# An attention and gated-MLP kernel on one core: query product units begin in odd blocks, their steps at other positions, and the score tiles stand ahead of the values while a unit holds a PSUM pair

## The chip, the core and the metric

The kernel runs on one core of a Trainium2 chip. A core has TensorE (matrix products into PSUM, its weights loaded by a separate queue that the profile calls PEld), VectorE (DVE), ScalarE (ACT), GpSimd (POOL) and SyncE (SP, which issues the transfers). Each engine takes its instructions in the order of the program and stops at one whose semaphore hasn't come yet. The metric is the device time of one execution in microseconds, lower is better. Times below are in microseconds from the first instruction of the profiled execution where they stand as positions.

## The reference

Two parts share a layer norm of `x` (2048 rows of 512). `A` is attention of 32 heads of 128 over a cache of 2048 keys, without a mask; `B` is a gated MLP with relu on the gate.

```python
def _A_ref(x, k_cache, v_cache, wq, wo):
    q = (x @ wq).reshape(B, Sq, H, Dh).transpose(0, 2, 1, 3)
    scores = jnp.einsum("bhqd,bhkd->bhqk", q, k_cache) * (Dh ** -0.5)
    p = _softmax(scores, axis=-1)
    o = jnp.einsum("bhqk,bhkd->bhqd", p, v_cache)
    return o.transpose(0, 2, 1, 3).reshape(B, Sq, H * Dh) @ wo

def _B_ref(x, W_gate, W_up, W_down):
    gate = x @ W_gate
    h = gate * (gate > 0) * (x @ W_up)
    return h @ W_down

xn = _layernorm(A_x)
out = A_x + _A_ref(xn, ...) * silu(_B_ref(xn, ...))
```

## The kernel before, in words

**The main loop.** The attention is cut into 128 *blocks*, one for each head and quarter of the queries (512 rows); `blk_of` gives block, head, quarter and *position*. A block has 8 positions, each a *pair* of key tiles (2 x 128 keys). For a pair, TensorE makes two score tiles (`emit_S_tile`, line 1461) into one PSUM pair, ScalarE takes the exponential of both in one instruction (line 1473) into `PT`, and later TensorE multiplies both tiles with the values (`emit_PV_tile`, line 1570, eight matmuls a pair) into the accumulator `ps_acc`. The values run three pairs behind the scores (`LAG`): an iteration of the loop opens pair `gp` and does the values of pair `gq = gp - 3`. At a block's end VectorE normalizes the accumulator (`emit_norm_block`, a reciprocal at line 1490 and a product at line 1493), and the next block's first value matmul waits for that.

**The ring.** Six PSUM banks, as three pairs, are handed out in turn by `ring_acquire` to pairs of score tiles and to side products. A pair comes back when the exponential has read it, or when VectorE has read a side product. `ring_acquire(hold=True)` takes a pair out of the turn, and `ring_release` puts it back as the next but one; meanwhile two pairs are left for the scores.

**Side products.** What else TensorE has to do is spread over the iterations by a plan written out by hand, `plan[(block, position)]`, and short pieces of other engines by `side[(block, position)]`. In an iteration with items of the plan, both score tiles come first, then the items, then the values. In one without, the order is score tile, half of the values, score tile, half of the values. Blocks in `early` have a product that takes only one bank at position 0; there the next pair's two score tiles are opened ahead of it as well, and position 1 opens none.

- *Output products* (`emit_os`, line 1342): the output projection of a finished group of four heads (16 blocks), as seven products for each of four quarters, spread over the 16 blocks of the next group, one step at position 0 of each. Each fourth step is a single bank; its blocks (3, 7, 11 and 15 of a group) are the early ones. VectorE adds the results to `s_acc` (line 1360).
- *Output sums* (`emit_ox`, lines 1311 to 1319): sums and differences of attention outputs that these products read, four VectorE operations each for the first half (`c = 0`, read from block 1 on) and the second half (`c = 1`, read from block 9 on). They are written into one buffer, `OX`.
- *Weight sums for them* (`emit_wx`, GpSimd): one scaling and four sums per group.
- *Query product units* (`emit_unit`, line 1027): the queries of head group `g` are made by two nested levels of a seven-product scheme, in the 16 blocks before they are used. A group has seven units (`j` = 1, 2, 6, 5, 3, 7, 4), each again of seven products in six steps. Steps 0 to 3 share one held pair of banks: step 0 makes two products, the others one; a step often waits for VectorE's result of the step before (`k["b"]`, `k["a"]`), since it accumulates on a bank that VectorE has just read. Steps 4 and 5 hold a pair again, in the next block. VectorE does two operations each for steps 0 and 1 and one for each of the others (lines 1031 and 1032); in step 1 of the units that add to a base (all but `j` = 1 and 5) the second is of double width, 128x1024. `prep_unit` makes a unit's operand sums on GpSimd (line 999) two blocks ahead, and `add_unit` adds two buffers on GpSimd after units 5 and 7.

`unit_at` lists where units begin: before, in blocks 6, 8, 10, 12, 14 of a group and 0 and 2 of the next (even blocks), with steps at positions 2, 4, 5, 6 of that block and 2, 4 of the next. There are units for six groups, from block 22 to block 115. The first two groups' queries are made by a simpler scheme, `emit_st`: its step 0 copies a product from PSUM to the buffer `cu` on VectorE (line 909).

Of the kernel before, what the change touches and what calls it, by code (L numbers as in the profile page):

```python
# [30 lines left out]
def _wait(eng, tok):  # L31
    if tok is None:
        return
    sem, val = tok
    if val <= 0:
        return
    eng.wait_ge(sem.h, val)


def _wait_all(eng, toks):  # L40
    best = {}
    for t in toks:
        if t is None:
            continue
        sem, val = t
        k = id(sem)
        if k not in best or best[k][1] < val:
            best[k] = (sem, val)
    for sem, val in best.values():
        _wait(eng, (sem, val))  # L50


def bass_recurrent_scan__mha_block_cached__glu_gated_reglu__prompt_kernel(
# [24 lines left out]
    NP = KT // 2  # L78
# [3 lines left out]
    NG = H // G  # L82
# [29 lines left out]
    act = nc.scalar  # L112
    dve = nc.vector
# [3 lines left out]
    with ExitStack() as es:  # L117
# [9 lines left out]
        def newsem(unit=1):  # L127
            _cnt[0] += 1
            return _Sem(es.enter_context(nc.semaphore(f"sem{_cnt[0]}")), unit)

        ps_r = P_([128, 2 * NSLOT, 512], F32, "ps_r")
# [136 lines left out]
        sem_g = newsem()  # L268
        sem_qpe = newsem()
        sem_da = newsem()  # L270
        sem_rz = newsem()
        sem_norm = newsem()
        sem_opa = newsem()
# [589 lines left out]
        GBK = G * QB  # L863
# [9 lines left out]
        st_tok = {}  # L873

        def emit_st(pr, c, step, *banks):
            W, X = Wq_sb[pr % 2], SW[pr % 2] if pr else SW0
            cu, cv = cuv0 if pr == 0 and c == 0 else cuv
            lo = slice(c * NQ, (c + 1) * NQ)
            hi = slice(HS + c * NQ, HS + (c + 1) * NQ)
            h0, h1 = 2 * pr, 2 * pr + 1  # L880
            Q0, Q1 = c, c + QB // 2

            def prod(k, bank):
                L, R = {
                    1: (lambda i: W[:, i, 0, :], lambda i: xnT[:, i, lo]),
                    2: (lambda i: W[:, HC + i, 0, :], lambda i: xnT[:, HC + i, lo]),
                    3: (lambda i: X[:, 3, i, :], lambda i: xnT[:, HC + i, hi]),
                    4: (lambda i: W[:, HC + i, 1, :], lambda i: TX[:, 3, i, lo]),
                    5: (lambda i: X[:, 0, i, :], lambda i: TX[:, 0, i, lo]),
                    6: (lambda i: X[:, 1, i, :], lambda i: TX[:, 1, i, lo]),  # L890
                    7: (lambda i: X[:, 2, i, :], lambda i: TX[:, 2, i, lo]),
                }[k]
                ins = None
                for i in range(HC):
                    ins = pe.matmul(ps_r[:, bank, :], L(i), R(i), start=(i == 0), stop=(i == HC - 1))  # L895
                return sem_qp.sig(ins)

            def comb(dst, a, bank, op=ALU.add, waits=()):
                _wait_all(dve, waits)
                return sem_qpe.sig(dve.tensor_tensor(dst, a, ps_r[:, bank, :], op))  # L900

            if step == 0:
                _wait(pe, sw_tok[(pr, 0)])
                if pr == 0 and c == 0:
                    _wait_all(pe, xt_ready[0])
                p1 = prod(1, banks[0])
                p2 = prod(2, banks[1])
                _wait(dve, p1)
                st_tok["u"] = sem_qpe.sig(dve.tensor_copy(cu[:], ps_r[:, banks[0], :]))
                r = qt_ready[(h0, Q0)] = comb(qt_take(h0, Q0), cu[:], banks[1], waits=(p2, st_tok["u"]))  # L910
                return [st_tok["u"], r]
            if step == 1:
                if c == 0:
                    _wait(pe, sw_tok[(pr, 1)])
                    _wait(pe, tx_tok[(1, 3)])
                p6 = prod(6, banks[0])
                p5 = prod(5, banks[1])
                st_tok["u"] = comb(cu[:], cu[:], banks[0], waits=(p6, st_tok["u"]))
                st_tok["v"] = comb(cv[:], cu[:], banks[1], waits=(p5, st_tok["u"]))
                return [st_tok["v"]]  # L920
            if step == 2:
                p3 = prod(3, banks[1])
                p7 = prod(7, banks[0])
                qt_ready[(h0, Q1)] = comb(qt_take(h0, Q1), cv[:], banks[1], waits=(p3, st_tok["v"]))
                st_tok["u"] = comb(cu[:], cu[:], banks[0], waits=(p7, st_tok["u"]))
                r = qt_ready[(h1, Q1)] = comb(qt_take(h1, Q1), cv[:], banks[0])
                return [r]
            p4 = prod(4, banks[0])
            if c == 1:
                qp_done_tok[pr] = p4  # L930
            r = qt_ready[(h1, Q0)] = comb(qt_take(h1, Q0), cu[:], banks[0], waits=(p4, st_tok["u"]))
            st_tok["r"] = r
            return [r]

        qp3 = {18: ((1, 0), (3, 1), (5, 2)), 19: ((0, 3), (2, 4), (4, 5)), 20: ((3, 6), (5, 7))}
        unit_at = [(g, j, GBK * (g - 1) + 6 + 2 * k) for g in range(2, NG)
                   for k, j in enumerate((1, 2, 6, 5, 3, 7, 4))]
        u_prep = {}
        u_done = {}
# [1 line left out]
        u_held = {}  # L941
# [699 lines left out]
        GB = G * QB  # L1641
        LB = NBLK - QB
        side = {}
        osteps = {}
        early = set()
        for g in range(NG - 1):
            b0 = (g + 1) * GB
            for i in range(16):
                it = (emit_os, 1 if i % 4 == 3 else 2, g, i // 4, i % 4)
                if g < NG - 2 or i < 10:  # L1650
                    osteps[b0 + i] = it
                else:
                    at(b0 + (10, 10, 11, 12, 13, 13)[i - 10], 4 * (i in (11, 15)), it)
            for c in range(2):
                for i in range(4):
                    side.setdefault((b0 + 7 * c, (2, 1)[c] + i), []).append((emit_ox, g, c, i))
        gu_n = [len(gu_seq)]

        def gu_items(n):
# [17 lines left out]
        for b in range(NBLK):  # L1677
            pr, r = (b - 2) // 8 + 1, (b - 2) % 8
# [22 lines left out]
            elif 0 < pr < NPR:  # L1701
                c, step = r // 4, r % 4
                q = (emit_st, 1 if step == 3 else 2, pr, c, step)
                first, second = (o, q) if step == 3 and o else (q, o)
# [3 lines left out]
            else:  # L1708
                assert not o
        for n, (g, j, b) in enumerate(unit_at):  # L1710
            for step, (r, p) in enumerate(((0, 2), (0, 4), (0, 5), (0, 6), (1, 2), (1, 4))):
                at(b + r, p, (emit_unit, 0, n, step))
            side.setdefault((b - 2, 0), []).append((prep_unit, n))
            if j in (5, 7):
                side.setdefault((b + 1, 5), []).append((add_unit, g, j))
        side.setdefault((GB + 1, 0), []).append((spill_g,))
        side.setdefault((LB - 9, 5), []).append((reload_g,))
        for g in range(2, NG):
            b = GB * (g - 1)
# [35 lines left out]
        for gp in range(LAG, TOTP):  # L1755
            gq = gp - LAG
            bq, hq, Qq, pq = blk_of(gq)
            items = plan.pop((bq, pq), None)
            b, h, Q, p = blk_of(gp)
            if p == 0 and Q == 0:  # L1760
                sp_head_start(h)
            ahead = gp in s_ahead
            if not ahead:
                open_S_pair(gp)
                emit_S_tile(gp, 0)
            if pq == 0 and bq % 8 == 4:
                pr = bq // 8 + 2
                if pr < 4:
                    _wait(sp, qp_done_tok[pr - 2])
                    issue_wq(pr)  # L1770
            if pq == 4 and bq % 8 == 4:
                pr = bq // 8 + 2
                if pr < 4:
                    emit_sw(pr)
            if pq == 0 and bq == (NG - 1) * GB + 4:
                _wait(sp, u_tok["last"])
                for k in range(4):
                    issue_xr(k)
            if pq == 4 and bq == 0:
                gu_sums(2)  # L1780
            if pq == 0 and bq == 13:
                emit_wx_scale(0)
            if pq == 0 and bq == GB:
                emit_wx(0)
            if pq == 0 and bq == GB + 3:
                emit_wx(1)
            if pq == 6 and bq % GB == 8 and 1 < bq // GB < NG - 1:
                emit_wx(bq // GB)
            if items:
                if not ahead:  # L1790
                    emit_S_tile(gp, 1)
                if pq == 0 and bq in early:
                    s_ahead.add(gp + 1)
                    emit_S_pair(gp + 1)
                for it in items:
                    emit_M(it)
            for fn, *args in side.pop((bq, pq), []):
                fn(*args)
            for fn in later.pop(gq, []):
                fn()  # L1800
            now[0] = gq + 1
            emit_PV_tile(gq, 0)
            if not items and not ahead:
                emit_S_tile(gp, 1)
            emit_PV_tile(gq, 1)

# [40 lines left out]
```

## Time and profile before

| | |
|---|---|
| time, median of 3 runs | 1265.59 us (1265.51 to 1265.65) |
| time of the profiled execution | 1265.56 us |
| its span, first to last instruction | 1264.2 us |
| TensorE clock granted | 0.999 |
| exponentials, line 1473 | 1024, mean 1029 ns, 982.6 us busy |
| value matmuls, line 1570 | 8192 |
| VectorE operations of units, 128x512, line 1032 | mean 685 ns |
| the same, double width 128x1024 | mean 1220 ns |
| additions to the output, line 1360 | 264, mean 683 ns |

In a row of the timeline the columns are: start, length, engine, line, operation, written tile <- read tiles, shapes, how many were merged; in brackets, how long the engine stood idle before it and who ended that. The idle time of PE is that against the ends of the records; a matmul's record goes on after the next one has begun, so a stall shows in the distance between starts, not in the bracket. In rows that list one group of instructions, the numbers are shortest, median and longest duration in ns, then the first and last start.

### The profile page before, as it was taken

How to read it: one execution, taken by the hardware profiler on the slowest of the kernel's cores; microseconds unless marked ns; L12 is line 12 of the kernel's file. 1: busy time of each engine (PE TensorE's matmuls, PEld its weight loads, DVE VectorE, ACT ScalarE, POOL GpSimd, SP SyncE). 2: the span in 40 equal slices, each digit the busy share in tenths (PEclk: the TensorE clock that was granted, in tenths of full speed). 3: DMA queues.
4: the chain of work that ended last, by engine and by line, in shares of the span. 5: the costliest groups of instructions: out<-in, count | busy, mean ns of one | idle time of the engine just before them, and what ended most of it. 6: DMA issues, size and time to landing. Idle time of an engine off the chain costs nothing.

```text
span 1264.2 us, 29137 instructions
## 1 busy us (share of the span) xinstructions
PE 1238.9 (98%) x12124; PEld 856.6 (68%) x12353; DVE 804.9 (64%) x1329; ACT 1033.6 (82%) x1108; POOL 588.5 (47%) x606
## 2 busy tenths in 40 slices
PE   9999999999999999999999999999999999999998
PEld 5466666776767676667766677767666676766775
DVE  7677887765566646664665646564655656565667
ACT  4457877668888898888888898888888898889994
POOL 3473876315525366254654457335645447430002
PEclk9999999999999999999999999999999999999999
DMA  9712331315212332323212223233223132235312
GB/s 271 154 31 43 71 80 29 45 43 126 39 35 48 75 60 47 51 64 68 52 37 47 53 60 51 51 64 67 48 51 65 30 56 47 51 66 140 76 35 76
DMA packets 254914, 82.25 MB, mean 65 GB/s; under 512 B 226368, under 2 KB 254784, under 8 KB 254784
## 3 DMA queue, kind: packets, MB, share of 16 engines
q1 hardware_dynamic: 254112, 79.98, 30.8%
q8 instruction: 98, 1.61, 0.5%
q10 hardware_dynamic: 672, 0.39, 0.1%
q14 instruction: 32, 0.26, 0.1%
HBM read 40.63 MB, written 4.19 MB: 35 GB/s over the span
## 4 chain that ended last, share of the span: by engine, by line
PE 80%; issue 8%; ACT 7%; DVE 3%; POOL 0%; DMA 0%; POOLq 0%; DVEq 0%
PE ps_acc L1570 31%; PE ps_r L1461 26%; ACT PT L1473 7%; PE ps_r L1027 6%; PE ps_r L1342 6%; PE ps_r L1139 3%; PE ps_r L1200 2%; PE ps_r L710 2%; PE ps_r L714 2%; PE ps_r L895 2%; DVE UVR L1032 1%; PE ps_acc L813 1%; POOL g_sb L1625 0%; DVE OX L1319 0%; DVE OX L1313 0%
## 5 line engine op out<-in xcount | busy, mean ns | idle before, releaser
L1473 ACT ACTIVATE PT<-ps_r 128x1024 bf16<-128x1024 f32 x1024 | 982.6, 1029 | 161.3 <-PE ps_r L1461 148.5
L1570 PEld LDWEIGHTS ps_acc<-V_sb,PT 128*128 128x128 bf16 x8192 | 589.2, 98 | 199.5 <-ACT PT L1473 2.9
L1570 PE MATMUL ps_acc<-V_sb,PT 128*128 128x129 bf16 x8192 | 715.7, 220 | 7.1
L1461 PE MATMUL ps_r<-QT_sb,KT_sb 128*128 128x512 bf16 x1835 | 626.1, 379 | 8.6 <-DVE UVR L1032 5.4
L1032 DVE TENSOR_TENSOR UVR<-UVR,ps_r 128x512 f32<-128x512 f32 (+1 forms) x228 | 168.2, 755 | 89.7 <-PE ps_r L1027 86.8
L1461 PEld LDWEIGHTS ps_r<-QT_sb,KT_sb 128*128 128x128 bf16 x2048 | 179.5, 98 | 14.2 <-DVE UVR L1032 5.1
L1360 DVE TENSOR_TENSOR s_acc<-s_acc,ps_r 128x512 f32<-128x512 f32 x264 | 167.8, 683 | 21.9 <-PE ps_r L1342 21.9
L1490 DVE RECIPROCAL rz_sb<-ps_acc 128x4 f32<-128x4 f32 x127 | 23.2, 182 | 217.0 <-PE ps_acc L1570 216.9
L999 POOL TENSOR_TENSOR TI<-xn_sb 128x512 f16<-128x512 f16 x48 | 55.3, 1153 | 113.3 <-PE ps_r L1027 113.3
L1493 DVE TENSOR_TENSOR Onorm<-ps_acc,rz_sb 128x512 bf16<-128x512 f32 x127 | 87.8, 691 | 4.4
L999 POOL TENSOR_TENSOR TI<-xnT 128x512 f16<-128x512 bf16 x36 | 41.5, 1154 | 69.6 <-PE ps_r L1027 68.8
L973 POOL TENSOR_SCALAR Wq_sb<-Wq_sb 128x1024 bf16<-128x1024 bf16 x12 | 33.2, 2768 | 83.5 <-DMA Wq_sb<-in_A_wq_dram 83.5
L1032 DVE TENSOR_TENSOR QT_sb<-UVR,ps_r 128x512 bf16<-128x512 f32 x72 | 47.9, 686 | 36.6 <-PE ps_r L1027 34.2
L1098 POOL TENSOR_TENSOR QT_sb<-UVR,UVR 128x512 bf16<-128x512 f32 x24 | 29.8, 1274 | 81.8 <-DVE UVR L1032 81.8
L1098 POOL TENSOR_TENSOR UVR<-UVR,UVR 128x512 f32<-128x512 f32 x24 | 29.8, 1272 | 73.3 <-DVE UVR L1032 73.3
L1625 POOL TENSOR_TENSOR g_sb<-s_acc,WX 128x512 bf16<-128x512 f32 x6 | 6.8, 1153 | 117.3 <-DVE WX L1618 117.3
L999 POOL TENSOR_TENSOR TI<-xn_sb,TI 128x512 f16<-128x512 f16 x48 | 55.4, 1154 | 0.0
L1027 PE MATMUL ps_r<-TI,SI 128*128 128x512 f16 x126 | 48.0, 381 | 0.6
L1342 PE MATMUL ps_r<-WX,OX 128*128 128x256 f16 x336 | 45.8, 273 | 0.0
L999 POOL TENSOR_TENSOR TI<-xnT,TI 128x512 f16<-128x512 bf16 x36 | 41.6, 1157 | 0.0
L1115 POOL TENSOR_SCALAR gB<-gB 128x512 bf16<-128x512 bf16 x14 | 20.8, 1487 | 42.4 <-DVE gB L1145 42.4
L1342 PEld LDWEIGHTS ps_r<-WX,OX 128*128 128x128 f16 x336 | 32.9, 98 | 9.8 <-ACT PT L1473 1.8
(185 smaller groups left out, 1191.2 us busy)
## 6 DMA issues: line engine op xcount, KB each, us to landing
V_sb<-in_A_v_cache_dram SPq DMA_DIRECT2D x32, 512.0 KB, 4.5
Wq_sb<-in_A_wq_dram SPq DMA_DIRECT2D x16, 256.0 KB, 3.1
Wo_sb<-in_A_wo_dram SPq DMA_DIRECT2D x8, 512.0 KB, 4.9
out_dram<-g_sb SPq DMA_DIRECT2D x4, 512.0 KB, 4.8
g_sb<-out_dram SPq DMA_DIRECT2D x4, 512.0 KB, 6.6
xr_sb<-in_A_x_dram SPq DMA_DIRECT2D x16, 128.0 KB, 2.2
OT_store<-Onorm SPq DMA_TRANSPOSE x127, 2.5
Wd_sb<-in_B_W_down_dram SPq DMA_DIRECT2D x1, 1792.0 KB, 14.6
```

The lines of the kernel that those rows point to most:

```text
L973: wu_tok[(g, i)] = sem_uo.sig(pool.tensor_scalar(w, w, WSC, None, op0=ALU.mult))
L999: return sem_ui.sig(pool.tensor_tensor(dst, x, y, o))
L1027: return sem_up.sig(pe.matmul(dst, lhs, rhs, start=start, stop=stop, skip_group_check=True))
L1032: dve.tensor_tensor(dst, x, ps, ALU.add))
L1098: u_tok["add"] = sem_uv.sig(pool.tensor_tensor(dst, UU[:, i, :], RR[:, i, :], ALU.add))
L1139: ins = pe.matmul(ps_r[:, bank, :], L(i), R(i), start=(i == 0), stop=(i == HC - 1))
L1342: ins = pe.matmul(ps_r[:, bank, j * DH:(j + 1) * DH], L(i), R(i), start=(i == 0 and j == 0), stop=(i == GH - 1 and j == 1))
L1360: t = dve.tensor_tensor(names[k], names[k], view(bank), op)
L1461: ins = pe.matmul(ps_r[:, 2 * s + tt, :], KT_sb[h % 2][:, t * 128:(t + 1) * 128], QT_sb[qt_slot[(h, Q)]][:], start=True, stop=True)
L1473: act.activation(PT[pb][:], ps_r[:, 2 * s:2 * s + 2, :], ACTF.Exp, scale=scale / WSC)
L1493: dve.tensor_tensor(Onorm[ob][:], o_ap, rz_sb[:].to_broadcast([128, 4, Dh]), ALU.mult))
L1570: ins = pe.matmul(o_ap, PT[pb][:, tt, j * 128:(j + 1) * 128], V_sb[vb][:, t, 0:VW], start=(t == 0 and j % 2 == 0), stop=(t == KT - 1 and j ...
```

## The change

Six edits to the order of work; no product is added or left out.

1. `emit_st`, step 0 of head pair 0, second column: the copy to `cu` is done by ScalarE, not VectorE (once in the program).
2. Units begin one block earlier, in odd blocks (5, 7, 9, 11, 13, 15 and 1).
3. Their first four steps are at positions 2, 3, 5, 6, or 3, 4, 6, 7 in early blocks, in place of 2, 4, 5, 6. The last two stay at 2 and 4 of the next block.
4. The output sums of the second half move from block 7, positions 1 to 4, to block 8, positions 2 to 5 (except in the last group).
5. `emit_wx` of group 1 comes a block later, those of later groups a block earlier.
6. In an iteration without items, both score tiles come ahead of the values while a unit holds a pair, and at position 7 ahead of an early block.

```diff
@@ emit_st, step 0
-                _wait(dve, p1)
-                st_tok["u"] = sem_qpe.sig(dve.tensor_copy(cu[:], ps_r[:, banks[0], :]))
+                if pr == 0 and c == 1:
+                    _wait_all(act, [p1, st_tok["r"]])
+                    st_tok["u"] = sem_qpa.sig(act.copy(cu[:], ps_r[:, banks[0], :]))
+                else:
+                    _wait(dve, p1)
+                    st_tok["u"] = sem_qpe.sig(dve.tensor_copy(cu[:], ps_r[:, banks[0], :]))
@@ 
-        unit_at = [(g, j, GBK * (g - 1) + 6 + 2 * k) for g in range(2, NG)
+        unit_at = [(g, j, GBK * (g - 1) + 5 + 2 * k) for g in range(2, NG)
                    for k, j in enumerate((1, 2, 6, 5, 3, 7, 4))]
@@ 
             for c in range(2):
                 for i in range(4):
-                    side.setdefault((b0 + 7 * c, (2, 1)[c] + i), []).append((emit_ox, g, c, i))
+                    side.setdefault((b0 + 7 * c, 1 + i) if c and g == NG - 2 else (b0 + 8 * c, 2 + i), []).append((emit_ox, g, c, i))
@@ 
         for n, (g, j, b) in enumerate(unit_at):
-            for step, (r, p) in enumerate(((0, 2), (0, 4), (0, 5), (0, 6), (1, 2), (1, 4))):
+            first = (3, 4, 6, 7) if b in early else (2, 3, 5, 6)
+            for step, (r, p) in enumerate([(0, p) for p in first] + [(1, 2), (1, 4)]):
                 at(b + r, p, (emit_unit, 0, n, step))
@@ the loop
-            if pq == 0 and bq == GB + 3:
+            if pq == 0 and bq == GB + 4:
                 emit_wx(1)
-            if pq == 6 and bq % GB == 8 and 1 < bq // GB < NG - 1:
+            if pq == 6 and bq % GB == 7 and 1 < bq // GB < NG - 1:
                 emit_wx(bq // GB)
...
+            split = not items and not ahead
+            if split and (u_held or (pq == NP - 1 and bq + 1 in early)):
+                emit_S_tile(gp, 1)
+                split = False
             emit_PV_tile(gq, 0)
-            if not items and not ahead:
+            if split:
                 emit_S_tile(gp, 1)
             emit_PV_tile(gq, 1)
```

`GB` and `GBK` are 16, the blocks of a group; `NG` is 8, the groups; `NP` is 8, the positions of a block; `u_held` holds the pairs that units hold at that moment.

More of the change, by code (lines that the diff above doesn't have):

```diff
@@ L270, in bass_recurrent_scan__mha_block_cached__glu_gated_reglu__prompt_kernel @@
         sem_da = newsem()
+        sem_qpa = newsem()
         sem_rz = newsem()
```

## The prediction

> **What bounds the kernel now.** I read the page first, then who waits for whom, then the timeline of single blocks.
>
> ```profile
> span 1264.2 us, 29137 instructions
> PE 1238.9 (98%) x12124; PEld 856.6 (68%) x12353; DVE 804.9 (64%) x1329; ACT 1033.6 (82%) x1108; POOL 588.5 (47%) x606
> ...
> PEclk9999999999999999999999999999999999999999
> ...
> PE 80%; issue 8%; ACT 7%; DVE 3%; POOL 0%; DMA 0%; POOLq 0%; DVEq 0%
> ```
>
> TensorE carries the time at a full clock. Its busy share hides stalls, since a record outlasts the gap to the next matmul, so I count by start times. Of a plain block (68):
>
> ```profile
> 733.25 1.04 PE L1342 MATMUL ps_r<-Wo_sb,OT_store 128*128 128x256 bf16 x8
> 734.12 0.62 PE L1570 MATMUL ps_acc<-V_sb,PT 128*128 128x129 bf16 x8
> 734.58 0.38 PE L1461 MATMUL ps_r<-QT_sb,KT_sb 128*128 128x512 bf16 x1
> 734.79 0.39 PE L1570 MATMUL ps_acc<-V_sb,PT 128*128 128x129 bf16 x4
> ...
> 736.35 0.38 PE L1461 MATMUL ps_r<-QT_sb,KT_sb 128*128 128x512 bf16 x1
> ```
>
> 734.58 to 736.35 is two pairs: 0.885 us a pair, of which a score tile takes 0.2165 and four value matmuls 0.226. An output product pair costs 0.865 (733.25 to 734.12), a single half of that; a unit's product is as wide as a score tile, 0.2165. Now one group of 16 blocks, by the normalizations (first and last of 17):
>
> ```profile
> L1490 DVE RECIPROCAL rz_sb<-ps_acc x17: 177/183/183, 696.6 to 836.5; 128x4 f32<-128x4 f32 x17
> ```
>
> 139.9 us. The work in it is 128 x 0.885 + 12 x 0.865 + 4 x 0.43 + 49 x 0.2165 = 136.0. So **3.9 us per group is stall**, some 23 us over the six groups with units: no reordering can bring more than that. Where it lies:
>
> First the collision in the first block of a group (block 64), TensorE and then VectorE:
>
> ```profile
> 702.37 0.59 PE L1461 MATMUL ps_r<-QT_sb,KT_sb 128*128 128x512 bf16 x2
> 703.24 0.39 PE L1027 MATMUL ps_r<-xn_sb,SI 128*128 128x512 f16 x1 [0.27 <-DVE UVR L1032]
> ...
> 705.83 0.39 PE L1570 MATMUL ps_acc<-V_sb,PT 128*128 128x129 bf16 x4
> 707.12 0.38 PE L1461 MATMUL ps_r<-QT_sb,KT_sb 128*128 128x512 bf16 x1 [0.90 <-DVE UVR L1032]
> ```
> ```profile
> 704.35 0.68 DVE L1316 TENSOR_TENSOR OX<-OX,OT_store 128x1024 f16<-128x1024 f16 x1
> 704.95 0.68 DVE L1032 TENSOR_TENSOR UVR<-UVR,ps_r 128x512 f32<-128x512 f32 x1
> 705.55 0.69 DVE L1319 TENSOR_TENSOR OX<-OT_store,OX 128x1024 f16<-128x1024 bf16 x1
> 706.15 0.68 DVE L1032 TENSOR_TENSOR UVR<-UVR,ps_r 128x512 f32<-128x512 f32 x1
> ```
>
> The output sums (OX) stand between the unit's own operations. The product at 703.24 was due at 702.80 (two score tiles after 702.37): 0.44. The score tile before 707.12 was due at 706.06 and began at 706.90, when the pair that the unit had held came free: 0.84. Together the collision costs **1.28** a group.
>
> Second, a unit's four first steps in any even block (66), and the block after:
>
> ```profile
> 720.60 0.38 PE L1027 MATMUL ps_r<-TI,SI 128*128 128x512 f16 x1
> 720.82 0.62 PE L1570 MATMUL ps_acc<-V_sb,PT 128*128 128x129 bf16 x8
> 721.31 0.59 PE L1461 MATMUL ps_r<-QT_sb,KT_sb 128*128 128x512 bf16 x2
> 721.76 0.39 PE L1027 MATMUL ps_r<-xn_sb,SI 128*128 128x512 f16 x1
> ...
> 723.01 0.39 PE L1027 MATMUL ps_r<-xn_sb,Wq_sb 128*128 128x512 f16 x1
> ...
> 724.14 0.38 PE L1461 MATMUL ps_r<-QT_sb,KT_sb 128*128 128x512 bf16 x1
> 724.35 0.39 PE L1570 MATMUL ps_acc<-V_sb,PT 128*128 128x129 bf16 x4
> 724.58 1.03 PE L1461 MATMUL ps_r<-QT_sb,KT_sb 128*128 128x512 bf16 x4
> 725.63 0.61 PE L1342 MATMUL ps_r<-WX,OT_store 128*128 128x256 f16 x4
> ```
> ```profile
> 721.02 1.94 DVE L1032 TENSOR_TENSOR UVR<-UVR,ps_r 128x512 f32<-128x512 f32 x2 [0.70 <-PE ps_r L1027]
> ```
> ```profile
> 724.55 2.85 ACT L1473 ACTIVATE PT<-ps_r 128x1024 bf16<-128x1024 f32 x3 [0.46 <-PE ps_r L1461]
> ```
>
> The fourth step (723.01) was due at 721.76 + 0.2165 + 0.45 + 0.433 = 722.87 and waits for VectorE's double-width operation, which ends at 722.96: 0.15, in the five units of a group that have a base. 721.31 should be 721.27, and 721.76 should be 721.74: with only two pairs left, the tile waits for an exponential that began late because its second score tile stands behind half of the values. With 0.04 in the next block that is 0.10 per unit. And in an early block four score tiles run together and the output product needs a third pair: due at 724.58 + 0.866 = 725.44, begun at 725.63, when the exponential of 724.55 (1.03 long) ends. Block 119, early without a unit, has it too:
>
> ```profile
> 1171.21 8.36 ACT L1473 ACTIVATE PT<-ps_r 128x1024 bf16<-128x1024 f32 x9 [0.52 <-PE ps_r L1461]
> ```
> ```profile
> 1176.55 1.03 PE L1461 MATMUL ps_r<-QT_sb,KT_sb 128*128 128x512 bf16 x4
> 1177.79 0.61 PE L1342 MATMUL ps_r<-WX,OT_store 128*128 128x256 f16 x4 [0.21 <-ACT PT L1473]
> ```
>
> (due 1177.42, so 0.37). Early blocks: 0.24 each, the 0.19 and what the single product loses after it. Sum: 1.28 + 5 x 0.15 + 7 x 0.10 + 4 x 0.24 = 3.7 of 3.9.
>
> The rows also give the latencies that I use: product to VectorE 0.42 (720.60 to 721.02), VectorE's end to TensorE 0.05 (722.96 to 723.01), second score tile to exponential 0.41 (724.14 to 724.55), exponentials in a row one per (8.36 - 1.02) / 8 = 0.917.
>
> **The change part by part.** Nothing is added to or taken from TensorE's work; all is waiting. Times below count from a block's first score tile.
>
> *Units begin in odd blocks.* The last unit of a group (j=4) now begins in the second block of the next one, so block 0 holds only the last two steps of j=7 beside the sums. That pairing exists already (block 71, sums among the last two steps):
>
> ```profile
> 761.33 0.68 DVE L1032 TENSOR_TENSOR UVR<-UVR,ps_r 128x512 f32<-128x512 f32 x1
> 761.93 0.69 DVE L1313 TENSOR_TENSOR OX<-OT_store 128x1024 f16<-128x1024 bf16 x1
> ...
> 763.73 1.15 DVE L1319 TENSOR_TENSOR OX<-OT_store,OX 128x1024 f16<-128x1024 bf16 x1
> 766.27 0.18 DVE L1490 RECIPROCAL rz_sb<-ps_acc 128x4 f32<-128x4 f32 x1 [1.40 <-PE ps_acc L1570]
> ```
>
> VectorE is idle 1.40 before the next normalization. So -1.28 per group. The second half of the sums moves to block 8 for the same reason, at the same price of zero: its readers come at the start of block 9. With the three output additions of a full product ahead of the sums, that idle shrinks to a few tenths.
> The operation at 763.73 took 1.15 where its like at 705.55 took 0.69. In the new places two of the four sums fall behind the unit's last step, which is also what releases GpSimd's next work: up to 2 x 0.46 a set, covered while the idle time lasts.
> The Trainium skill (GPSIMD Engine Reference, 1. Specifications) speaks against the move: GpSimd shares its SBUF interfaces with VectorE operations that have two SBUF inputs. The trace agrees, with that 1.15 against 0.69.
>
> *Steps at 2, 3, 5, 6.* Third and fourth step now come two rounds after the double-width operation: it ends at about 6.85, the fourth step is at 7.53. -5 x 0.15. In exchange the second step is directly behind the first: products at 3.07 and 3.28, VectorE on the second from 3.70 to 4.39, so the second step can begin at 4.44; TensorE is there at 3.28 + 0.2165 + 0.45 + 0.433 = 4.38. **+0.06 a unit**, 7 a group (bounds: nothing, and the 0.15 of 723.01).
>
> *Score tiles together while a pair is held.* The exponential begins 0.23 earlier, so the pair for two rounds later is free in time: the 0.10 per unit goes, -0.70. Order costs nothing: a round with both tiles ahead costs what its tiles cost (720.60 to 720.82 is 0.22).
>
> *The same ahead of an early block.* Here I expect nothing. That block is now preceded by one whose steps lie at 2 and 4, so its last three rounds are plain, 0.885 each against 0.917 for ScalarE. Position 5's second tile is at 6.16, its exponential runs from 6.58 to 7.60, and position 7's ends at 7.60 + 2 x 0.917 = 9.44 in either order; the product may begin at 9.49 and is due at 8.375 + 0.866 = 9.24. 0.25 in place of 0.19: **+0.05** for 4 blocks a group (between -0.24 and the 0.37 of block 119).
>
> *Steps at 3, 4, 6, 7 in early blocks.* Three units a group. The last product ends the block; VectorE is done with it 0.42 + 0.69 later, so the held pair comes free 1.16 after it. The next block's output product takes that pair and is due 0.2165 + 0.45 + 0.433 = 1.10 after: 0.06. The normalization queues behind, then the additions, then the next hold: another 0.03. **+0.09**, 3 a group (between nothing and the 0.84 of 707.12).
>
> *Earlier preparation, sums and weights on GpSimd.* Same order of the queue, and the first operation of a preparation is released by TensorE:
>
> ```profile
> 763.17 1.15 POOL L999 TENSOR_TENSOR TI<-xn_sb 128x512 f16<-128x512 f16 x1 [11.20 <-PE ps_r L1027]
> ```
>
> 11.2 us idle before it, its eight operations 6.5 us: nothing. SyncE's loads keep their places.
>
> *The copy on ScalarE* (once, at the loop's start):
>
> ```profile
> 71.83 1.02 ACT L1473 ACTIVATE PT<-ps_r 128x1024 bf16<-128x1024 f32 x1 [0.70 <-PE ps_r L1461]
> ...
> 72.26 0.69 DVE L909 COPY cuv<-ps_r 128x512 f32<-128x512 f32 x1 [0.17 <-PE ps_r L895]
> ...
> 73.06 0.69 DVE L900 TENSOR_TENSOR QT_sb<-cuv,ps_r 128x512 bf16<-128x512 f32 x1
> ```
>
> VectorE waited 0.17 for this product, so its queue was not what held it; ScalarE is free for it only about 0.92 after 71.83, at 72.75. Ended at 73.35, the next operation begins 0.3 late, and the later exponentials 0.1: **+0.3** (bounds: -0.69, the copy's length, and +0.5).
> The Trainium skill (Perfetto Trace Analysis, Optimizing Scalar/DVE Operations) would offload a saturated VectorE to ScalarE; by that the sum is 1.0 better. The 0.17 of idle speaks against it.
>
> **Sum.** A full group: -1.28 - 0.75 - 0.70 + 0.42 + 0.20 + 0.27 = -1.84; five of them -9.2. The first (blocks 21 to 31: five units' 0.10 and three 0.15 against six 0.06, three 0.05, two 0.09) -0.3. The last (blocks 112 to 115: 1.28 + 2 x 0.15 + 2 x 0.10 against 0.2) -1.6; block 115 also loses a 0.2 stall of that kind in which a unit's product met the last output sums. Together -11.3, with the copy -11.0. The profiled execution took 1264.2 and 1.4 around it, 1265.6, which is the median too: **1254.5 us**, own range 1252 to 1257.
>
> **The rivals.**
> *The early stall goes too* (0.10). If exponentials in the block before don't run in a row, the tile 0.23 earlier is worth the whole 0.24: 25 early blocks, -6, 1248.5. For it: the change names exactly these blocks. Against: the nine in a row before block 119.
> *The sums slowed by GpSimd reach the normalization* (0.13). Sets in blocks 0 and 8 end about 8.5, the normalization wants VectorE at 8.6. 12 to 13 sets x 0.5 = +6: 1260.5. For it 763.73; against it the few tenths of cover.
> *The held pair comes back late* (slower, 0.08). After steps that end at position 7 the very next output product needs that pair, and TensorE stands in order behind it. If VectorE is a whole operation or more behind there, the price is 707.12's 0.84 in place of 0.09, 18 times: +13.5, 1268. It makes the whole slower from 11 / 18 = 0.6 us each. Against it: nothing but the unit uses VectorE from position 3 on.
> *All cancels* (0.04): several of the bounds at once, within 0.2%, about what a measurement can tell from no change.
>
> **How the numbers follow.** Likeliest 0.65, the rivals as given. The range 1248 to 1261 takes in the first two and the bounds of the +0.06 and +0.05 terms; it leaves out 0.12 to 0.2. Faster by over 0.2% is 0.65 + 0.10 + 0.13 = 0.88, same 0.04, slower 0.08.
>
> **What would show it.** Block 0 of a group: no wait of 0.4 or more on UVR, and the group at 138.0 to 138.2 instead of 139.9. In units: no wait at the fourth step, one of 0.06 at the second. The single output product of early blocks still waiting 0.2 to 0.3 for an exponential. I am wrong if a wait for VectorE over 0.3 stands before the output product of the block after an early one, if OX runs into the normalization, or if the early stall is gone.

## The result, and the profile after

The changed kernel takes **1254.22 us** (median of 4 runs, 1254.09 to 1254.29); the kernel before took 1265.62 beside it (1265.51 to 1265.71). The ratio is 0.991, with a 95% interval of 0.9893 to 0.9927: 11.4 us. The forecast was 1254.5. The head of the changed kernel's page and its shares of the chain:

```profile
span 1252.9 us, 29140 instructions
PE 1233.0 (98%) x12125; PEld 857.2 (68%) x12353; DVE 811.0 (65%) x1328; ACT 1033.4 (82%) x1109; POOL 596.2 (48%) x606
...
PE 80%; ACT 10%; issue 8%; DVE 1%; POOL 0%; DMA 0%; POOLq 0%; DVEq 0%
```

The span lost 11.3. No work went away (one copy changed engines). VectorE's share of the chain fell from 3% to 1% and ScalarE's rose from 7% to 10%: where the chain leaves TensorE, it now goes mostly through ScalarE. The normalizations of the same group as in the prediction (line 1490 is 1495 now), the first and the last of 17:

```profile
L1495 DVE RECIPROCAL rz_sb<-ps_acc x17: 172/183/184, 693.9 to 831.9; 128x4 f32<-128x4 f32 x17
```

A group takes 138.0 in place of 139.9. Now the places that the prediction named. Block 0 of the group (block 64), first on TensorE, then on VectorE; the products at 696.71 and 698.70 are the last two steps of unit 7:

```profile
693.76 0.38 PE L1466 MATMUL ps_r<-QT_sb,KT_sb 128*128 128x512 bf16 x1
694.04 1.05 PE L1347 MATMUL ps_r<-Wo_sb,OT_store 128*128 128x256 bf16 x8
...
696.71 0.38 PE L1032 MATMUL ps_r<-TI,SI 128*128 128x512 f16 x1
...
698.70 0.38 PE L1032 MATMUL ps_r<-TI,SO 128*128 128x512 f16 x1
```
```profile
697.13 0.69 DVE L1037 TENSOR_TENSOR UVR<-UVR,ps_r 128x512 f32<-128x512 f32 x1 [0.54 <-PE ps_r L1032]
697.73 0.69 DVE L1316 TENSOR_TENSOR OX<-OT_store 128x1024 f16<-128x1024 bf16 x1
...
699.11 0.69 DVE L1037 TENSOR_TENSOR UVR<-UVR,ps_r 128x512 f32<-128x512 f32 x1
...
700.44 1.65 DVE L1324 TENSOR_TENSOR OX<-OT_store,OX 128x1024 f16<-128x1024 bf16 x1
702.22 0.18 DVE L1495 RECIPROCAL rz_sb<-ps_acc 128x4 f32<-128x4 f32 x1
```

Both steps come on time, between sums that nobody waits for: the waits of 0.44 and 0.84 are gone. The output product at 694.04 was due at 693.98 (a score tile after 693.76); those 0.06 are the held pair that comes back late. The last sum took 1.65, beside GpSimd's additions after unit 7 (below), and ended 0.13 before the normalization; the next output product wasn't held up by it.

The second step of a unit (block 69), and the output product of an early block (67) with the exponentials before it:

```profile
739.25 0.59 PE L1466 MATMUL ps_r<-QT_sb,KT_sb 128*128 128x512 bf16 x2
739.74 0.39 PE L1032 MATMUL ps_r<-TI,SI 128*128 128x512 f16 x1
```
```profile
719.56 1.03 PE L1466 MATMUL ps_r<-QT_sb,KT_sb 128*128 128x512 bf16 x4
720.67 0.61 PE L1347 MATMUL ps_r<-WX,OT_store 128*128 128x256 f16 x4
```
```profile
717.76 4.69 ACT L1478 ACTIVATE PT<-ps_r 128x1024 bf16<-128x1024 f32 x5 [0.20 <-PE ps_r L1466]
```

739.74 was due at 739.25 + 0.433 = 739.68: 0.06. 720.67 was due at 719.56 + 0.866 = 720.42: 0.25; the third of the five exponentials in a row ends just ahead of it, at 720.61.

### The profile page after: what moved, and what is told of

The parts are those of the page before. It is cut to its first block, busy times and chain, and to the rows that moved or that the text cites. A ratio compares the mean times of both kernels' runs of the same rounds, so it can differ in the third digit from the quotient of the medians.

```text
span 1252.9 us, 29140 instructions
## 1 busy us (share of the span) xinstructions
PE 1233.0 (98%) x12125; PEld 857.2 (68%) x12353; DVE 811.0 (65%) x1328; ACT 1033.4 (82%) x1109; POOL 596.2 (48%) x606
## 4 chain that ended last, share of the span: by engine, by line
PE 80%; ACT 10%; issue 8%; DVE 1%; POOL 0%; DMA 0%; POOLq 0%; DVEq 0%
PE ps_acc L1575 31%; PE ps_r L1466 25%; ACT PT L1478 10%; PE ps_r L1347 6%; PE ps_r L1032 6%; PE ps_r L1144 3%; PE ps_r L1205 3%; PE ps_r L711 2%; PE ps_r L715 2%; PE ps_r L896 2%; PE ps_acc L814 1%; POOL g_sb L1630 0%; DMA x_sb<-in_A_x_dram 0%; PE ps_r L528 0%; DVE stats L406 0%
## 5 line engine op out<-in xcount | busy, mean ns | idle before, releaser
L1575 PEld LDWEIGHTS ps_acc<-V_sb,PT 128*128 128x128 bf16 x8192 | 579.3, 98 | 202.4 <-ACT PT L1478 2.9
L1575 PE MATMUL ps_acc<-V_sb,PT 128*128 128x129 bf16 x8192 | 697.9, 220 | 5.6
L1466 PE MATMUL ps_r<-QT_sb,KT_sb 128*128 128x512 bf16 x1834 | 613.0, 379 | 5.0 <-DVE QT_sb L901 0.3
L1466 PEld LDWEIGHTS ps_r<-QT_sb,KT_sb 128*128 128x128 bf16 x2048 | 175.6, 98 | 7.6 <-ACT PT L1478 0.5
L1004 POOL TENSOR_TENSOR TI<-xn_sb 128x512 f16<-128x512 f16 x48 | 58.0, 1209 | 68.0 <-PE ps_r L1032 68.0
L1103 POOL TENSOR_TENSOR QT_sb<-UVR,UVR 128x512 bf16<-128x512 f32 x24 | 34.8, 1481 | 72.7 <-DVE UVR L1037 72.7
```

Of the source, the lines that this page charges most:

```text
L1004: return sem_ui.sig(pool.tensor_tensor(dst, x, y, o))
L1103: u_tok["add"] = sem_uv.sig(pool.tensor_tensor(dst, UU[:, i, :], RR[:, i, :], ALU.add))
L1466: ins = pe.matmul(ps_r[:, 2 * s + tt, :], KT_sb[h % 2][:, t * 128:(t + 1) * 128], QT_sb[qt_slot[(h, Q)]][:], start=True, stop=True)
L1575: ins = pe.matmul(o_ap, PT[pb][:, tt, j * 128:(j + 1) * 128], V_sb[vb][:, t, 0:VW], start=(t == 0 and j % 2 == 0), stop=(t == KT - 1 and j ...
```

## The experiments

The blocks of two runs are compared by the start of the last value matmul of each, so a gain or loss has a place. All times are medians beside runs of the kernel before on the same chip (1265.61 to 1265.68).

### The order of score tiles: is it the exponential's early start?

The loop's edit has two halves: position 7 ahead of an early block, and every iteration without items while a pair is held. Take away each:

```
-            if split and (u_held or (pq == NP - 1 and bq + 1 in early)):
+            if split and u_held:                               # after_no_p7
+            if split and pq == NP - 1 and bq + 1 in early:     # after_no_held
```

> The changed kernel, but at position 7 ahead of an early block the values stand between the score tiles again; all else as changed. My theory: that part of the change is worth nothing in this layout, since ScalarE's exponentials run in a row before an early block and the tile's order doesn't move them: 1254.2 us, within 0.3, and the single output product of early blocks waits 0.25 us as in the changed kernel. Rival (the early part removes a stall that would else be there): slower by up to 25 x 0.24 = 6 us, 1260.

Measured 1254.25, ratio 0.9911 (0.9898 to 0.9925): no difference from the change. Position 7 alone is worth nothing here, as forecast.

> The changed kernel, but while a unit holds a pair the values stand between the score tiles again (the part at position 7 stays). The prediction's term: the order takes away 0.10 us per unit, so it comes back: 42 x 0.10 = 4.2, 1258.4 us. Rival A: the new positions of the steps took most of it away themselves; walked through, only the block of the last two steps loses 0.04 (the exponential of its third round ends at 5.62 instead of 5.46, and the tile of its fifth is due at 5.72): 42 x 0.04 = 1.7, 1255.9. Rival B: nothing, 1254.2.

Measured 1255.56, ratio 0.9922 (0.9909 to 0.9934): +1.3 where the prediction's term said +4.2. The blocks with a unit's last two steps are 0.04 longer and nearly all others unchanged. One of them, block 66, without the held part, TensorE and then ScalarE:

```profile
717.09 0.62 PE L1575 MATMUL ps_acc<-V_sb,PT 128*128 128x129 bf16 x8
717.58 0.38 PE L1466 MATMUL ps_r<-QT_sb,KT_sb 128*128 128x512 bf16 x1
```
```profile
714.43 5.04 ACT L1478 ACTIVATE PT<-ps_r 128x1024 bf16<-128x1024 f32 x5 [0.70 <-PE ps_r L1466]
```

The tile at 717.58 was due at 717.54, after eight value matmuls (0.45): that 0.04 is the tile waiting for an exponential, the third of the five in this row. It runs from 716.41 to 717.44, having started 0.41 after its second score tile (716.00), which stands behind half of the values again. The 0.06 in the unit's first block, which the prediction had put down to the same cause, does not come back. To see where it was, the loop's edit alone in the kernel before, without any of the others:

```
+            split = not items and not ahead
+            if split and (u_held or (pq == NP - 1 and bq + 1 in early)):
+                emit_S_tile(gp, 1)
+                split = False
             emit_PV_tile(gq, 0)
-            if not items and not ahead:
+            if split:
                 emit_S_tile(gp, 1)
```

> The kernel before with one edit alone: both score tiles ahead of the values while a pair is held, and at position 7 ahead of an early block. My theory: while held, 42 x 0.10 = 4.2 us less. Ahead of early blocks, the steps of the old layout at 4, 5 and 6 leave ScalarE idle (0.46 us before the exponential at 724.55), so here the tile 0.23 earlier takes the whole 0.19 wait of the output product away: 24 blocks, 4.5 us less; block 119 stays. Together 1265.6 - 8.7 = 1256.9. Rival A: only the held part works, 1261.4. Rival B: the order is worth nothing and the positions do all of it, 1265.6.

Measured 1258.66, ratio 0.9946 (0.9933 to 0.9958), 7.0 better than before. Block 66 and the early block 67 on TensorE, then VectorE in 66 (lines as before the change):

```profile
717.63 0.62 PE L1570 MATMUL ps_acc<-V_sb,PT 128*128 128x129 bf16 x8
718.09 0.59 PE L1461 MATMUL ps_r<-QT_sb,KT_sb 128*128 128x512 bf16 x2
718.58 0.39 PE L1027 MATMUL ps_r<-xn_sb,SI 128*128 128x512 f16 x1
...
721.40 1.03 PE L1461 MATMUL ps_r<-QT_sb,KT_sb 128*128 128x512 bf16 x4
722.26 0.60 PE L1342 MATMUL ps_r<-WX,OT_store 128*128 128x256 f16 x4
```
```profile
717.83 1.94 DVE L1032 TENSOR_TENSOR UVR<-UVR,ps_r 128x512 f32<-128x512 f32 x2 [0.70 <-PE ps_r L1027]
```

Against the prediction's rows, the score tile is on time (718.09, 0.45 after 717.63; it had been 0.04 late), but the third step is now 0.06 late (718.58, due 718.52) where it had been 0.02. The end of the block does not move. The third step waits for the first of VectorE's two operations: 0.42 from product to VectorE, 0.69 of work, 0.05 back, 1.16 in all. Between products of neighbouring rounds TensorE has 0.2165 + 0.45 + 0.433 = 1.10 of work. **So two steps in neighbouring rounds, of which one waits for a single VectorE operation on the product of the other, cost 0.06 here**; the late tile had only used up part of that time.

The second finding is the early block: its output product is on time at 722.26 (721.40 + 0.866), and these blocks are 0.26 shorter. These blocks also hold a unit's last two steps, whose 0.04 is seen alone in blocks 9 and 13. So in the old layout position 7 was worth some 24 x 0.22 = 5.3 of the 7.0, and the blocks of the last two steps 42 x 0.04 = 1.7; this split is worked out from the block lengths, position 7 alone was not run in that layout. The same line is worth 0 in the new layout, where three plain rounds come ahead of the early block.

### The steps' positions

```
-            first = (3, 4, 6, 7) if b in early else (2, 3, 5, 6)
+            first = (2, 4, 5, 6)
```

> The changed kernel with the first four steps of every unit at positions 2, 4, 5, 6 again, still in odd blocks. By the prediction's terms: 30 units with a base wait 0.15 us again (+4.5), 42 units lose the 0.06 behind their first step (-2.6), and in 18 early blocks the held pair comes back in time for the next output product (18 x 0.09, -1.6): +0.3, 1254.5. Rival (the new positions are a large part of the gain, and what they cost is small): the 4.5 alone, 1258.7.

Measured 1257.79, ratio 0.9937 (0.9924 to 0.9949): +3.6, against +0.3. Blocks 9 and 13, whose units have a base, lose 0.15 each, as the 0.15 of the fourth step said. The 0.06 that the second step should give back is not gained, because the second and third are now the neighbours. The third step of block 69, a unit without a base:

```profile
742.79 0.59 PE L1466 MATMUL ps_r<-QT_sb,KT_sb 128*128 128x512 bf16 x2
743.28 0.39 PE L1032 MATMUL ps_r<-xnT,SI 128*128 128x512 bf16 x1
```

743.28 was due at 743.22. Of early blocks 7 and 15 each loses 0.21 and the block behind gains 0.16 and 0.09. A group loses 0.53. So the fourth step's wait was rightly priced, and the turnaround between neighbours was not won or lost but moved.

### The sums and GpSimd

The change moves two things that could meet: the sums (OX) go from block 7 to 8, and GpSimd's weight sums from block 8 to 7. Put the sums back alone, put the weight sums a block behind both places (9) alone, and do both:

```
-  (b0 + 7 * c, 1 + i) if c and g == NG - 2 else (b0 + 8 * c, 2 + i)
+  (b0 + 7 * c, 1 + i) if c else (b0, 2 + i)               # after_sums7, sums7_weights9
-            if pq == 6 and bq % GB == 7 and 1 < bq // GB < NG - 1:
+            if pq == 6 and bq % GB == 9 and 1 < bq // GB < NG - 1:   # after_weights9, sums7_weights9
```

> The changed kernel with the output sums of the second half back in block 7, positions 1 to 4, where now a unit's first steps stand (positions 3, 4, 6, 7). My theory: the sums push VectorE's operations of the unit back by 0.6 to 0.7, its last one ends about 10.0 us after the block's first score tile, and the output product of block 8, due at 9.34, waits for the held pair: about 0.7 us per group, six groups, 1254.2 + 4.2 = 1258.4. Rival (the sums cost nothing wherever they stand, the gain of block 0 came from the unit's new place alone): 1254.2.

Measured **1278.23**, ratio 1.0099 (1.0083 to 1.0114): 24 us slower than the change, and slower than before, where 4 were expected. It lies in one place of each of five groups. VectorE, GpSimd and TensorE in block 71:

```profile
765.94 4.11 DVE L1318 TENSOR_TENSOR OX<-OT_store 128x1024 f16<-128x1024 bf16 x1
769.98 1.27 DVE L1037 TENSOR_TENSOR UVR<-UVR,ps_r 128x512 f32<-128x512 f32 x2
```
```profile
765.56 5.69 POOL L1289 TENSOR_SCALAR Wo_sb<-Wo_sb 128x2048 bf16<-128x2048 bf16 x1
```
```profile
766.98 0.59 PE L1466 MATMUL ps_r<-QT_sb,KT_sb 128*128 128x512 bf16 x2
770.71 0.61 PE L1032 MATMUL ps_r<-TI,SI 128*128 128x512 f16 x1 [3.14 <-DVE UVR L1037]
```

A sum that usually takes 0.68 began 0.38 after GpSimd's scaling of the weights and took 4.11. The unit's operations stand behind it, and TensorE waits 3.3 for them (due 766.98 + 0.433). Then it is slow as well. Three of its stretches (start and end, length, busy time of PE, PEld, DVE, ACT and POOL, granted clock, DMA share, GB/s):

```profile
770.20:770.70 0.50, 0.00 (x0) 0.00 (x0) 0.50 (x2) 0.00 (x0) 0.50 (x1) 0.50 1.28 292
772.50:773.55 1.05, 1.05 (x8) 0.77 (x8) 1.05 (x1) 0.48 (x1) 1.05 (x2) 0.50 0.00 0
773.65:774.00 0.35, 0.35 (x5) 0.21 (x3) 0.35 (x2) 0.35 (x1) 0.35 (x2) 1.00 0.00 0
```

Half the clock, until some 3 us after the matmuls resume. Four of the five groups lose 4.6 to 4.9 in this way. In the third (block 55) TensorE waits the same 3.3 (625.41 to 628.71) and the clock stays at 1.00; that group loses 4.0, of which 3.2 in block 55 and 0.7 in block 56. Beside it, the half clock made only 0.6 to 0.9 of the loss of the others.

> As the kernel with the sums back in block 7 (1278.2 us, a sum of 4.11 us while GpSimd scales the output weights), but GpSimd's scaling and sums of the output weights are queued two blocks later, at block 9, position 6, behind the preparation of the next unit. Theory A (the 4.1 us are the sum and the scaling at the same time): the sums take 0.7 to 1.2 again, the 3.3 us wait in block 7 and the half clock behind it go, and what is left is the collision with the unit's own operations, 0.7 per group: 1258.4. Theory B (the sums among the first steps do it by themselves): 1278.

Measured 1257.38, ratio 0.9935 (0.9922 to 0.9947): some 21 of the 24 us are the meeting with GpSimd, and what the sums alone cost in block 7 is 3.2, some 0.5 a group (0.7 expected). Line 1318 over this whole run, shortest, median and longest, shows the meeting gone:

```profile
L1318 DVE TENSOR_TENSOR OX<-OT_store x14: 678/680/685, 279.7 to 1173.4; 128x1024 f16<-128x1024 bf16 x14
```

In the run with the sums alone moved the same row reads 678/684/4115.

> The changed kernel, with GpSimd's scaling and sums of the output weights at block 9, position 6 alone. Control for the run with the sums in block 7: in the changed kernel the scaling ends before the sums of block 8 begin, so neither place touches them and nothing should change: 1254.2. If GpSimd's work in block 8 costs something in the changed kernel after all, this is faster.

Measured 1254.18, ratio 0.9911 (0.9895 to 0.9926): no difference. With the sums in block 8 the weight sums may come ahead of them or behind them.

### The copy on ScalarE

```
-                if pr == 0 and c == 1:
+                if False:
```

> The changed kernel with the one copy back on VectorE. The prediction's term says that the copy on ScalarE costs 0.3 us: 1253.9. The trace of the changed kernel shows the operation after it 0.38 later, but the sum operation behind that 0.79 long instead of 1.16, and the first two blocks together no longer than before, so the rival is no difference: 1254.2. A second rival (VectorE relieved of 0.69) would give 1254.9.

Measured 1254.23, ratio 0.991 (0.9895 to 0.9926): no difference. VectorE with the copy on ScalarE (the change), and GpSimd beside it:

```profile
73.44 0.69 DVE L901 TENSOR_TENSOR QT_sb<-cuv,ps_r 128x512 bf16<-128x512 f32 x1 [1.35 <-ACT cuv L911]
74.05 0.79 DVE L785 TENSOR_TENSOR HS_sb<-hT 128x1024 f16<-128x1024 f16 x1
74.87 1.04 DVE L788 TENSOR_TENSOR hT<-hT 128x1024 f16<-128x1024 f16 x1
```
```profile
73.62 0.67 POOL L623 TENSOR_TENSOR SG<-W,SG 128x256 f16<-128x256 bf16 x1
```

The same two operations in the kernel before:

```profile
73.66 1.16 DVE L784 TENSOR_TENSOR HS_sb<-hT 128x1024 f16<-128x1024 f16 x1
```
```profile
73.60 0.67 POOL L622 TENSOR_TENSOR SG<-W,SG 128x256 f16<-128x256 bf16 x1
```

The combination (line 901) begins 0.38 later than the 73.06 of before, close to the 0.3 worked out. But the operation after it took 0.79 and had taken 1.16 before, so the third begins at 74.87 in place of 74.85. What ends this operation is not its start but the GpSimd operation that it began beside: it ends 0.55 after that one before (74.27, 74.82), in the change (74.29, 74.84) and in this run (75.16, 75.70). Beginning 0.38 later cost nothing, since it would have stood still for that time.

### Score tiles ahead in every round, and the first step's products swapped

If the early product waits because exponentials run in a row through plain rounds, all of these rounds must be reordered, not only position 7. And if the second step waits 0.06 for the first step's second product, that product can come first.

```
-            if split and (u_held or (pq == NP - 1 and bq + 1 in early)):
+            if split:                        # after_all_ahead, after_all_ahead_swap
@@ emit_unit, step 0                          # after_all_ahead_swap
-            p1 = mm(A, ...)
-            p6 = mm(B, ...)
+            p6 = mm(B, ...)
+            p1 = mm(A, ...)
```

> The changed kernel with both score tiles ahead of the values in every iteration without items. My theory of the 0.25 us wait in early blocks: ScalarE runs in a row from the tile of position 5 on, whose exponential starts 0.23 late because the values stand between its score tiles. With position 5 and 6 ahead as well it runs from 6.35 to 7.38, position 7's ends at 9.21 and the output product can begin at 9.27 where it is due at 9.24: 24 blocks x 0.22, and 0.2 in block 119: 5.5 us less, 1248.7. Rival (three pairs are too few for four score tiles and an output product, whatever the order): 1254.2. A cost of the order itself would show as a plain pair over 0.885 us.

Measured 1248.28, ratio 0.9861 (0.9848 to 0.9875): -0.23 in every early block and nothing elsewhere. Early block 67, TensorE and ScalarE:

```profile
716.84 1.03 PE L1466 MATMUL ps_r<-QT_sb,KT_sb 128*128 128x512 bf16 x4
717.73 0.61 PE L1347 MATMUL ps_r<-WX,OT_store 128*128 128x256 f16 x4
```
```profile
710.85 8.66 ACT L1478 ACTIVATE PT<-ps_r 128x1024 bf16<-128x1024 f32 x9 [0.70 <-PE ps_r L1466]
```

The product waits 0.02 in place of 0.25. ScalarE now runs nine in a row; in the change it ran four, stood 0.20 until position 5's second score tile had come (the bracket of the row of 717.76), and ran five. With that tile 0.23 earlier its exponential and those behind it are earlier as well.

> As the kernel with both score tiles ahead everywhere, and in a unit's first step the product on which the second step waits is made first. My theory: the second step's wait of 0.06 us goes in 42 units, 2.6 us: 1246.1. Rival (VectorE's second operation then sets the second step's wait, or the wait moves to the third step): 1248.7.

Measured **1245.80**, ratio 0.9842 (0.9829 to 0.9856), 8.4 better than the change: the fastest version. In block 69:

```profile
735.16 0.59 PE L1466 MATMUL ps_r<-QT_sb,KT_sb 128*128 128x512 bf16 x2
735.59 0.38 PE L1032 MATMUL ps_r<-TI,SI 128*128 128x512 f16 x1
```

The second step comes 0.43 after 735.16, on time. The first blocks of six of a group's seven units are 0.07 shorter; that of the unit begun in block 1, whose wait is another (below), is not.

## Why the prediction was right, point by point

- **Sum.** A full group was to gain 1.84 and gained 1.86; it was to end at 138.0 to 138.2 and ended at 138.0. Right, though two of its terms were not what they were called. The forecast was off by 0.3, as much as the term of the copy, which measured nothing.
- **Collision in block 0, -1.28.** Right: no step there waits. Blocks 0 and 1 together, which share the unit that moved, went from 18.94 to 17.63. Block 115's stall of 0.2 is gone too. No run moves the units alone; this rests on the rows and the block lengths.
- **Fourth step, -5 x 0.15.** Right: with the old positions blocks 9 and 13 lost just that.
- **Second step directly behind the first, +0.06.** Right in size, 0.06 in the row above. In the unit that now begins in block 1 it is 0.11, because GpSimd's additions after unit 7, the one before it, still hold the buffer:

```profile
699.88 5.80 POOL L1103 TENSOR_TENSOR QT_sb<-UVR,UVR 128x512 bf16<-128x512 f32 x4 [12.11 <-DVE UVR L1037]
```
```profile
705.77 3.14 DVE L1037 TENSOR_TENSOR UVR<-UVR,ps_r 128x512 f32<-128x512 f32 x4 [1.40 <-PE ps_r L1032]
```

  They end at 705.68, and VectorE starts 0.04 later than the 705.73 that 0.42 after its product (705.31) gives.
- **Score tiles together while a pair is held, -0.10.** The step that failed. Only the 0.04 in the block of the last two steps is the exponential that began late. The 0.06 in the first block was VectorE's turnaround between the second and third step, which the order of tiles cannot shorten: that edit alone won nothing in those blocks. They fell away because the third step no longer stands directly behind the second, while the second step's +0.06 came in. So -0.42 and +0.42 a group are one wait that moved. The total came out right by luck: what the order did not give, the new positions gave. The rows of 721.31 and 721.76 showed a late tile and a late step; that removing the first would leave the second was not asked.
- **The same ahead of an early block, nothing; +0.05.** Right: 0.25 in place of 0.19, and the edit is worth 0 there. The rival of 1248.5 had the size of the stall right: with the tiles ahead in all rounds it goes, -6. Its condition did not hold, since ScalarE then runs nine in a row.
- **Steps at 3, 4, 6, 7, +0.09.** About right: blocks 0 and 12 are 0.10 longer than blocks 2 and 6, of which 0.06 at the output product. Block 8 is 0.17 longer, of which 0.13 there, since VectorE's last operation came 0.07 late:

```profile
761.04 0.38 PE L1032 MATMUL ps_r<-xnT,Wq_sb 128*128 128x512 bf16 x1
...
761.71 0.59 PE L1466 MATMUL ps_r<-QT_sb,KT_sb 128*128 128x512 bf16 x2
762.27 1.05 PE L1347 MATMUL ps_r<-Wo_sb,OT_store 128*128 128x256 bf16 x8
```
```profile
761.53 0.69 DVE L1037 TENSOR_TENSOR QT_sb<-UVR,ps_r 128x512 bf16<-128x512 f32 x1 [0.37 <-PE ps_r L1032]
```

  0.42 after 761.04 is 761.46. This operation writes finished queries, and all 54 of that kind in this trace that wait for their product and one other semaphore begin 0.49 after the product: a fixed 0.07 that the prediction did not have, not a buffer that came late. In the program the other semaphore is that of the freed query buffer; that this second wait makes the 0.07 was not tried. The rival in which VectorE is an operation or more behind (1268) did not happen.
- **Sums and GpSimd.** The slower sums are there, 1.65 in block 0, and 1.07 and 0.80 in block 8, where VectorE then stood idle for 0.53 before the normalization. VectorE, and the GpSimd operation that the first of them began beside:

```profile
768.03 1.07 DVE L1321 TENSOR_TENSOR OX<-OX,OT_store 128x1024 f16<-128x1024 f16 x1
769.13 0.80 DVE L1324 TENSOR_TENSOR OX<-OT_store,OX 128x1024 f16<-128x1024 bf16 x1
770.46 0.18 DVE L1495 RECIPROCAL rz_sb<-ps_acc 128x4 f32<-128x4 f32 x1 [0.53 <-PE ps_acc L1575]
```
```profile
767.40 1.15 POOL L1004 TENSOR_TENSOR TI<-xn_sb 128x512 f16<-128x512 f16 x1 [1.31 <-PE ps_r L1032]
```

  Covered, as forecast. But the price of 0.46 for such a meeting was a price for one neighbour. Every sum of this trace that took over 0.7 ends 0.55 after the GpSimd operation that it began beside (769.10 and 768.55 here), so the price is what that operation still has to run; beside the 128x2048 scaling it is 3.4. The weight sums may move to block 7 only if the output sums leave it.
- **Copy, +0.3.** The delay was 0.38, its effect 0: the next operation had been standing still for that time beside GpSimd. The term asked when the copy's result comes, and not what the operation behind it waits for.

## What to carry to other kernels

Count stalls by the starts of instructions on the engine that carries the time, and before crediting an edit with one, ask which wait ends second: the wait between neighbouring dependent steps was not removed here by moving them, only put between two others; it went when the product that the next step waits on was made first. The worth of an order edit belongs to its layout: one line was worth about 5 us before (an estimate from block lengths), nothing after, and 6 us once applied to all rounds. Before moving a VectorE operation with two SBUF inputs, look for GpSimd's longest operation near its new place and price the meeting by what that one still has to run.

## What the runs showed of the hardware

- A VectorE sum of two SBUF tiles, 128x1024 of 16 bits, took 0.68 alone, 1.65 beside GpSimd's f32 additions, and 4.11 when it began 0.38 after a 128x2048 GpSimd scaling. Beside GpSimd's sums of two tiles it ended 0.55 after the record of the one that had begun first, in the kernels before and after alike. The Trainium skill (SBUF — State Buffer, SBUF: two separate sides) says that whichever of the two starts first has the shared ports for its whole instruction, and the other blocks. The trace agrees in the main: the sum ended at 770.05 and GpSimd's record at 771.25, so it was held long but, by the records, not to the very end.
- In the run with the sums alone moved, TensorE's granted clock fell to 0.5 within 2.8 of the last matmul's end (767.41 to 770.20) and came back between 773.55 and 773.65, about 3.4 after the drop. By the trace's clock records this happened four times, from 486.90, 770.20, 913.56 and 1056.92, each time for 3.413. The distances between the drops are 83, 42 and 42 times 3.413: the clock changes on a fixed grid that does not start with the pause. In the 3.413 before each drop TensorE had 0.2 to 1.1 of work. The fifth pause, as long, fell across a line of this grid (626.84), with 2.0 and 1.5 of work in the two stretches that it touched, and the clock stayed. The Trainium skill (TensorE: Matmul & The Clock Gate, What's actually happening) gives a free-running window of 3.413 us and half the clock after at least one idle window. The grid and the way back agree; the drops do not need a wholly idle window here, since up to 1.1 of its 3.413 was work.
